# Linear attention plus SwiGLU, first four tiles: another way to transpose tiles 2 and 3, and query products summed by quarters

## The chip, the cores and the metric

The kernel runs on one core of one Trainium2 chip. A core has five engines that run side by side, each from a list of instructions of its own: TensorE (PE, matmuls and the loads of its weights, PEld), VectorE (DVE), ScalarE (ACT), GpSimd (POOL) and SyncE (SP, which here only issues DMA transfers). They wait for each other with semaphores. The metric is the device time in microseconds (us). The kernel before took 210.95 us (median of three runs, 210.83 to 211.18).

## The reference

Input x has 2048 rows of 512 numbers (bf16). It is normalised by rows, and the same normalised rows feed two blocks whose outputs are added to x.

```python
def _layernorm(x, axis=-1, eps=1e-5):
    m = jnp.mean(x, axis=axis, keepdims=True)
    v = jnp.var(x, axis=axis, keepdims=True)
    return (x - m) / jnp.sqrt(v + eps)

def _A_ref(x, wqkv, wo):                       # 32 heads of 16
    qkv = (x @ wqkv).reshape(B, S, 3, H, Dh).transpose(2, 0, 3, 1, 4)
    q, k, v = qkv[0], qkv[1], qkv[2]
    phi = lambda t: jnp.where(t > 0, t + 1, jnp.exp(t)) + 1e-6
    pq, pk = phi(q), phi(k)
    kv = jnp.einsum("bhsd,bhse->bhde", pk, v)
    z = jnp.einsum("bhsd->bhd", pk)
    num = jnp.einsum("bhqd,bhde->bhqe", pq, kv)
    den = jnp.einsum("bhqd,bhd->bhq", pq, z)[..., None] + 1e-6
    return (num / den).transpose(0, 2, 1, 3).reshape(B, S, D) @ wo

def _B_ref(x, w_gate, w_up, w_down):           # 1792 hidden
    return (jax.nn.silu(x @ w_gate) * (x @ w_up)) @ w_down

xn = _layernorm(x)
out = x + _A_ref(xn, A_wqkv, A_wo) + _B_ref(xn, B_w_gate, B_w_up, B_w_down)
```

## The kernel before, in words

The rows are cut into 16 tiles of 128, called tile 0 to 15, and the 512 columns into four chunks of 128. For the attention the kernel never forms V: it sums G = xnᵀ·phi(K) over all tiles in four PSUM banks (4 to 7) and multiplies by the V weights once at the end.

For each tile t the usual path is as follows. VectorE takes mean and variance (`bns`, L296, and `agg`, L299). 1/sqrt(var + eps) comes from two tiny operations, `eps` (L343, POOL or VectorE) and `rstd_of` (L352, POOL). `xn_dve` (L332) writes the normalised tile. A DMA transpose issued by SP (`transpose_dma`, L423) turns it, so that TensorE can use it as weights. `kproj` and `qproj` (L432) make K and Q, four matmuls of 512 columns each, into PSUM banks: bank 0 holds K and bank 1 holds Q of the even tiles, banks 2 and 3 those of the odd ones. ScalarE takes exp of K and of Q and copies Q out; VectorE clips exp K (L488) and adds max(K, 0) (L497), which gives phi(K). `gtacc` (L573) then adds xnᵀ·phi(K), four matmuls, to banks 4 to 7, and POOL adds phi(K) into a running sum (`zsum`, L565).

Tiles 0, 1 and 2 take another path, so that TensorE can begin early. Their rows are only centred (x minus mean, `xc_half` L379 or `xc_full` L389), the centred tile is transposed into `xcT`, and 1/sqrt is applied later as the scale of the ScalarE operations that read the products: `first_ek` (L505, exp), `first_pk` (L511, relu) and `first_pq` (L523, copy of Q). Scaling by a positive number per row after the product is the same as before it. Tiles 0 and 1 are transposed on TensorE against an identity (`tp_first`, L407: two transposes for half a tile, then one ScalarE copy from PSUM, L416). Tile 2 is transposed by a DMA (`transpose_xc`, L398). `proj_first` (L446) multiplies half the chunks at a time: halves 0 and 1 hold chunks 0, 1 and 2, 3. phi(K) of these tiles is the sum of two SBUF tensors, on POOL for tile 0 (`feat_pool`, L530) and on VectorE for tiles 1 and 2 (`first_feat`, L537). Exp of Q of tiles 0 to 2 is made in iterations 11 to 13 (`late_eq`, L517), and their normalised tiles are transposed by DMA in iterations 7 to 9, for the feed-forward block.

The order of the work is written out by hand. Every helper appends one operation to the list of its engine, with the semaphores that its inputs and outputs need, so the order of the calls is the order on each engine, and an operation that waits holds up everything behind it on that engine. Lines 593 to 700 hold the order for tiles 0 to 4, and a loop over tiles 5 to 15 the rest; then come the 56 steps of the feed-forward block (`ffn`, L753, gate and up products) with the attention's last products and the output tiles (L925 and L936) between them. TensorE starts with eight matmuls on constants (`fill`, L268). Loads are issued from SP in the order x 0, wk chunks 0 and 1, wk 2, x 2, wq 0, wq 1, x 3, wq 2, wq 3, x 4, x 5, and from ScalarE's queue x 1 and wk 3; x 6 to 15 follow in pairs.

Of the kernel before, what the change touches and what calls it, by code (L numbers as in the profile page):

```python
# [7 lines left out]
ALU = mybir.AluOpType  # L8
AX = mybir.AxisListType

P = 128
# [97 lines left out]
def bass_parallel_sum__linear_attn_block__swiglu_ffn__prompt_kernel(  # L109
# [16 lines left out]
    with contextlib.ExitStack() as es:  # L126
# [7 lines left out]
        xc_sb = sb("xc_sb", [3, D])  # L134
        xcT = sb("xcT", [3 * NDC, P])
# [123 lines left out]
        xload("sp", sp, 5, 1)  # L259

# [40 lines left out]
        def mean_act(t):  # L301
            K.op(
                "act",
                lambda: act.activation(
                    scr[:, :], x_sb[:, t, :], ACT.Copy, scale=1.0 / D, accum_out=mact[:, t, :],
                ),
                r=[("x", t)], w=[("mact", t), ("scr",)],
            )

        def negmean(t):  # L310
            K.op(
                "pool",
                lambda: pool.tensor_scalar(
                    out=nb[:, t:t + 1], in0=mv[:, t, 0:1], scalar1=rstd[:, t:t + 1], scalar2=-1.0,
                    op0=ALU.mult, op1=ALU.mult,
                ),
                r=[("mv", t), ("rstd", t)], w=[("nb", t)],
            )

        def xn_act(t):  # L320
            K.op(
                "act",
                lambda: act.activation(
                    xn_sb[:, t, :], x_sb[:, t, :], ACT.Identity, scale=rstd[:, t:t + 1], bias=nb[:, t:t + 1],
                ),
                r=[("x", t), ("nb", t), ("rstd", t)], w=[("xn", t)],
            )
# [74 lines left out]
        def tp_first(t, h, b):  # L402
# [10 lines left out]
            )  # L413
            K.op(
# [26 lines left out]
        def proj_first(t, wname, h):  # L441
# [10 lines left out]
                r=[("xcT", t, h)] + [(wname, i) for i in ((2, 3) if h else (0, 1))], w=[bk(b)],  # L452
            )
# [49 lines left out]
        def first_ek(t):  # L503
            K.op(
                "act", lambda: act.activation(ek[:, t, :], banks[kb(t)], ACT.Exp, scale=rstd[:, t:t + 1]),  # L505
                r=[bk(kb(t)), ("rstd", t)], w=[("ek", t)],
            )

        def first_pk(t):
            K.op(  # L510
                "act", lambda: act.activation(kpos[:, t, :], banks[kb(t)], ACT.Relu, scale=rstd[:, t:t + 1]),  # L511
                r=[bk(kb(t)), ("rstd", t)], w=[("kpos", t)],
            )
# [13 lines left out]
        def feat_pool(t):  # L527
            K.op(
                "pool",
                lambda: pool.tensor_tensor(out=pkq[:, t, 0, :], in0=kpos[:, t, :], in1=ek[:, t, :], op=ALU.add),  # L530
                r=[("kpos", t), ("ek", t)], w=[("pk", t)],
            )

        def first_feat(t):
            K.op(
                "dve",
                lambda: dve.tensor_tensor(out=pkq[:, t, 0, :], in0=kpos[:, t, :], in1=ek[:, t, :], op=ALU.add),  # L537
                r=[("kpos", t), ("ek", t)], w=[("pk", t)],
# [55 lines left out]
        stat(0)  # L594
        negmean(0)
        mean_act(1)
        xc_half(0, 0)
        tp_first(0, 0, 4)
        xc_half(0, 1)
        tp_first(0, 1, 5)  # L600
        fill(1, P)
        xc_half(1, 0, mact[:, 1, :], "mact")
        tp_first(1, 0, 6)
        xc_half(1, 1, mact[:, 1, :], "mact")
        tp_first(1, 1, 7)
        proj_first(0, "wk", 0)
        proj_first(0, "wk", 1)
        first_ek(0)
        bns(1)
        agg(1)  # L610
        eps(1, "pool")
        bns(2)
        agg(2)
        xc_full(2)
        proj_first(1, "wk", 0)
        proj_first(1, "wk", 1)
        first_pk(0)
        rstd_of(1)
        first_ek(1)
        clip_k(0)  # L620
        proj_first(0, "wq", 0)
        feat_pool(0)
        bns(3)
        agg(3)
        eps(3, "dve")
        rstd_of(3)
        proj_first(1, "wq", 0)
        xn_act(0)
        proj_first(0, "wq", 1)
        first_pq(0)  # L630
        bns(4)
        agg(4)
        eps(4, "pool")
        proj_first(1, "wq", 1)
        xn_dve(3)
        clip_k(1)
        xn_dve(1)
        gtacc(0)
        transpose_xc(2)
        proj_first(2, "wk", 0)  # L640
        proj_first(2, "wk", 1)
        xload("sp", sp, 6, 2)
        proj_first(2, "wq", 0)
        proj_first(2, "wq", 1)
        first_pk(1)
        first_feat(1)
        gtacc(1)
        rstd_of(4)
        xn_dve(4)
        bns(5)  # L650
        agg(5)
        first_pq(1)
        eps(2, "pool")
        rstd_of(2)
# [3 lines left out]
        transpose_dma(3)  # L658
        kproj(3)
        qproj(3)  # L660
        rstd_of(5)
        transpose_dma(4)
        xload("sp", sp, 8, 2)
        xn_dve(2)
        first_pk(2)
        first_feat(2)
        gtacc(2)
        xn_dve(5)
        xload("sp", sp, 10, 2)
        bns(6)  # L670
        exp_k(3)
        clip_k(3)
        agg(6)
        eps(6, "pool")
        rstd_of(6)
        transpose_dma(5)
        xload("sp", sp, 12, 2)
        xload("sp", sp, 14, 2)
        zsum(0, 0)
        bns(7)  # L680
        first_pq(2)
        copy_q(3)
        maxadd_k(3)
        kproj(4)
        xn(6)
        exp_k(4)
        qproj(4)
        agg(7)
        eps(7, "pool")
        exp_q(3)  # L690
        rstd_of(7)
        exp_q(4)
        copy_q(4)
        clip_k(4)
        stat(8)
        xn(7)
        zsum(1, 1)
        maxadd_k(4)
        stat(9)
# [6 lines left out]
        for t in range(5, NT):  # L706
# [12 lines left out]
            if t in (7, 8, 9):  # L719
                transpose_dma(t - 7)  # L720
# [6 lines left out]
            if t in (11, 12, 13):  # L727
                late_eq(t - 11)
# [304 lines left out]
```

## Time and profile before

| what | value |
|---|---|
| runs, device time | 210.83, 210.95, 211.18 us (median 210.95) |
| the profiled execution's own time | 210.89 us |
| its span, first to last instruction | 209.7 us |
| TensorE busy | 206.7 us (99%), 983 matmuls and transposes |
| VectorE, ScalarE, POOL busy | 119.4 (57%), 70.2 (33%), 74.4 (35%) us |
| share of the last chain of work on TensorE | 95% |
| granted TensorE clock, mean | 1.0 |

Rows of the timeline read: start and length in us, engine (PE, PEld, DVE, ACT, POOL, or a queue such as SPq that issues a DMA), line of the kernel, operation, output<-inputs, partitions x elements and type, xcount of like instructions in a row, and in brackets the idle time of the engine before them with what ended it. Lengths of matmuls overlap in time, because one starts before the last of the one ahead has drained: what one costs is read from the starts of two neighbours. For a DMA the issue is the row, and the landing is told apart from it.

### The profile page before, as it was taken

To read this page: it belongs to the slowest core of one execution; us is meant where nothing else is said; L and a number is where in the kernel's file an instruction comes from. 1 tells how busy PE (TensorE), PEld (TensorE's weight loads), DVE (VectorE), ACT (ScalarE), POOL (GpSimd) and SP (SyncE) were. 2 spreads that over 40 slices of the span, in tenths; PEclk is the share of its full clock that TensorE was granted. 3 is DMA by queue.
4 is the path that set the end of the run, shared out by engine and by line. 5 is a ranking of instruction groups with operands and counts; after the bars stand their busy time and mean duration, and the time that the engine had idled before them with its cause. 6 is when DMAs were issued, how large, how long until landed. Compare 5 with 4: busy or idle time off the path is not lost.

```text
span 209.7 us, 2763 instructions
## 1 busy us (share of the span) xinstructions
PE 206.7 (99%) x983; PEld 94.7 (45%) x983; DVE 119.4 (57%) x243; ACT 70.2 (33%) x123; POOL 74.4 (35%) x96
## 2 busy tenths in 40 slices
PE   8999999999999999999999999999999999999996
PEld 3344444445444444444444444444444444444444
DVE  4899988336265774637355746365556535373222
ACT  5957667956633331302122312213031213121000
POOL 3648987567032443223141422240424132221200
DMA  6766344894791111010202110202021010410201
GB/s 204 196 182 172 69 88 100 276 363 138 218 347 34 22 28 26 27 25 28 50 2 50 25 28 25 50 0 50 4 49 25 27 25 25 49 30 27 50 25 53
DMA packets 30287, 16.84 MB, mean 80 GB/s; under 512 B 20928, under 2 KB 29632, under 8 KB 30272
## 3 DMA queue, kind: packets, MB, share of 16 engines
q1 hardware_dynamic: 29984, 16.39, 29.6%
q10 hardware_dynamic: 288, 0.26, 0.4%
q8 instruction: 8, 0.13, 0.3%
q14 instruction: 7, 0.06, 0.1%
HBM read 9.70 MB, written 2.10 MB: 56 GB/s over the span
## 4 chain that ended last, share of the span: by engine, by line
PE 95%; DMA 2%; SPq 2%; issue 0%; DVE 0%
PE psum L753 46%; PE psum L936 23%; PE psum L432 11%; PE psum L925 7%; PE psum L573 7%; DMA wqkv_sb<-in_A_wqkv_dram 2%; PE psum L446 1%; SPq L211 1%; SPq L204 1%; PE psum L851 0%; PE psum L874 0%; DVE out_sb L949 0%
## 5 line engine op out<-in xcount | busy, mean ns | idle before, releaser
L768 ACT ACTIVATE sg<-psum 128x512 bf16<-128x512 f32 x56 | 33.4, 598 | 106.8 <-PE psum L753 104.9
L753 PE MATMUL psum<-xnT,wg_sb 128*128 128x512 bf16 x224 | 57.5, 379 | 0.0
L753 PE MATMUL psum<-xnT,wu_sb 128*128 128x512 bf16 x224 | 57.5, 379 | 0.0
L883 POOL TENSOR_TENSOR prod<-pkq,zb 128x512 f32<-128x512 bf16 x16 | 18.6, 1161 | 57.7 <-DVE pkq L497 57.7
L753 PEld LDWEIGHTS psum<-xnT,wu_sb 128*128 128x128 bf16 x224 | 21.9, 98 | 26.4
L753 PEld LDWEIGHTS psum<-xnT,wg_sb 128*128 128x128 bf16 x224 | 21.9, 98 | 26.2
L949 DVE TENSOR_TENSOR out_sb<-psum,x_sb 128x512 bf16<-128x512 f32 (+2 forms) x17 | 11.2, 660 | 35.5 <-PE psum L936 35.5
L907 POOL TENSOR_TENSOR pqn<-pkq,rden 128x512 bf16<-128x512 bf16 x16 | 16.9, 1056 | 36.9 <-DVE rden L901 36.9
L774 DVE TENSOR_TENSOR pkq<-psum,sg 128x512 bf16<-128x512 f32 x28 | 19.1, 687 | 18.5 <-PE psum L753 14.0
L774 DVE TENSOR_TENSOR xn_sb<-psum,sg 128x512 bf16<-128x512 f32 x28 | 18.8, 673 | 14.9 <-PE psum L753 14.4
L936 PE MATMUL psum<-wd_sb,xn_sb 128*128 128x512 bf16 (+2 forms) x126 | 25.7, 355 | 0.0
L936 PE MATMUL psum<-wd_sb,pkq 128*128 128x512 bf16 x112 | 25.5, 379 | 0.0
L432 PE MATMUL psum<-wqkv_sb,xnT 128*128 128x512 bf16 x104 | 24.4, 379 | 0.0
L565 POOL TENSOR_TENSOR zacc<-zacc,pkq 128x512 f32<-128x512 f32 x15 | 17.3, 1156 | 5.0 <-DVE ek L488 4.6
L936 PEld LDWEIGHTS psum<-wd_sb,xn_sb 128*128 128x128 bf16 x126 | 11.8, 98 | 12.5
L936 PEld LDWEIGHTS psum<-wd_sb,pkq 128*128 128x128 bf16 x112 | 11.0, 98 | 13.2
L925 PE MATMUL psum<-m_sb,eq 128*128 128x512 bf16 (+2 forms) x68 | 16.6, 366 | 0.0
L573 PE MATMUL psum<-pkq,xn_sb 128*128 128x512 bf16 x64 | 16.1, 379 | 0.0
L432 PEld LDWEIGHTS psum<-wqkv_sb,xnT 128*128 128x128 bf16 x104 | 10.1, 98 | 12.3 <-ACT ek L505 0.3
L891 DVE TENSOR_REDUCE den<-prod 128x32 f32<-128x512 f32 x16 | 10.9, 684 | 5.4 <-POOL prod L883 5.3
L296 DVE BATCH_NORM_STATS2 stats<-x_sb 128x6 f32<-128x512 bf16 x16 | 10.9, 683 | 3.3 <-DMA x_sb<-in_A_x_dram 3.3
L497 DVE SCALAR_TENSOR_TENSOR pkq<-pkq,eq 128x512 bf16<-128x512 bf16 x16 | 11.1, 693 | 0.6
(65 smaller groups left out, 136.7 us busy)
## 6 DMA issues: line engine op xcount, KB each, us to landing
out_dram<-out_sb SPq DMA_DIRECT2D x15, 128.0 KB, 1.7
wg_sb<-in_B_w_gate_dram SPq DMA_DIRECT2D x2, 896.0 KB, 7.8
wu_sb<-in_B_w_up_dram SPq DMA_DIRECT2D x2, 896.0 KB, 6.1
wd_sb<-in_B_w_down_dram SPq DMA_DIRECT2D x1, 1792.0 KB, 9.8
x_sb<-in_A_x_dram SPq DMA_DIRECT2D x5, 256.0 KB, 3.0
x_sb<-in_A_x_dram SPq DMA_DIRECT2D x5, 128.0 KB, 3.3
wqkv_sb<-in_A_wqkv_dram SPq DMA_DIRECT2D x5, 128.0 KB, 3.5
wqkv_sb<-in_A_wqkv_dram SPq DMA_DIRECT2D x1, 512.0 KB, 7.8
```

The lines of the kernel that those rows point to most:

```text
L432: (lambda c=c: pe.matmul(banks[b], xnT[:, c, t * P:(t + 1) * P], wqkv_sb[:, c, lo:lo + D], start=(c == 0), stop=(c == NDC - 1),))
L497: lambda: dve.scalar_tensor_tensor(out=dst, in0=src, scalar=0.0, in1=e, op0=ALU.max, op1=ALU.add,),
L565: lambda: pool.tensor_tensor(out=zacc[:, :], in0=zacc[:, :], in1=pk, op=ALU.add),
L573: (lambda c=c: pe.matmul(banks[4 + c], xn_sb[:, t, c * P:(c + 1) * P], pkq[:, t, 0, :], start=(t == 0), stop=(t == NT - 1),))
L753: (lambda c=c: pe.matmul(banks[b], w_sb[:, c, fc * P:(fc + 1) * P], xnT[:, c, C * 512:(C + 1) * 512], start=(c == 0), stop=(c == NDC - 1),))
L768: lambda: act.activation(sg[:, j % NSG, :], banks[gb], ACT.Silu),
L774: lambda: dve.tensor_tensor(out=hT(C, fc), in0=banks[ub], in1=sg[:, j % NSG, :], op=ALU.mult,),
L883: lambda: pool.tensor_tensor(out=p, in0=pkq[:, t, 1, :], in1=zb[:, :], op=ALU.mult),
L907: lambda: pool.tensor_tensor(out=pqn[:, t % NPN, :].rearrange("p (h e) -> p h e", e=DH), in0=pkq[:, t, 1, :].rearrange("p (h e) -> p h e", ...
L925: (lambda g=g: pe.matmul(dst, pqnT(t)[:, g, :], m_sb[:, g, lo:hi], start=(g == 0), stop=False,))
L936: (lambda fc=fc: pe.matmul(dst, hT(C, fc)[:, jj * P:(jj + 1) * P], wd_sb[:, fc, lo:hi], start=False, stop=(fc == NFC - 1),))
L949: lambda: dve.tensor_tensor(out=o, in0=src, in1=x_sb[:, t, lo:hi], op=ALU.add),
```

## The change

It touches the written-out order of tiles 0 to 4 and some helpers.

- Tile 3 goes the way of tiles 0 to 2: centred, transposed by DMA into `xcT`, multiplied with `proj_first`, its 1/sqrt applied by `first_ek`, `first_pk`, `first_pq`. Its normalised tile is still made, and its DMA transpose moves to iteration 6 of the loop; its exp of Q moves to iteration 14.
- Tile 2 is transposed on TensorE (banks 4 and 5) instead of by DMA. The ScalarE copy becomes a helper of its own (`tc_first`).
- Q 0 and Q 1, and K 0 and K 1, are issued one matmul at a time (`proj_part`): K by chunks 0, 1, 3, 2. After chunks 0 and 1 of Q 1 and of Q 0 stand the four transposes of tile 2, then chunk 2 of Q 0 and Q 1, chunk 3 of Q 0 and, behind it, chunk 3 of Q 1.
- Tile 0 is normalised on VectorE instead of ScalarE, and the small product on POOL for its bias goes.
- The load of x 6 and 7 is issued right behind x 5, before any transpose. `gtacc` 0 moves behind Q 2, `gtacc` 1 and 2 behind K 3, and the order on ScalarE, VectorE and POOL changes with them.

```diff
-        xc_sb = sb("xc_sb", [3, D])
-        xcT = sb("xcT", [3 * NDC, P])
+        xc_sb = sb("xc_sb", [4, D])
+        xcT = sb("xcT", [4 * NDC, P])
...
         xload("sp", sp, 5, 1)
+        xload("sp", sp, 6, 2)
...
+        def tc_first(t, h, b):
+            tb = banks[b].bitcast(bf)[:, 0:HD].rearrange("p (c s) -> p c s", c=2)
             K.op(
                 "act",
                 lambda: act.activation(xcT[:, NDC * t + 2 * h:NDC * t + 2 * h + 2, :], tb, ACT.Copy),
...
+        def proj_part(t, wname, c, pos):
+            lo, b = (D, kb(t)) if wname == "wk" else (0, qb(t))
+            K.op(
+                "pe",
+                lambda: pe.matmul(
+                    banks[b], xcT[:, NDC * t + c, :], wqkv_sb[:, c, lo:lo + D],
+                    start=(pos == 0), stop=(pos == NDC - 1),
+                ),
+                r=[("xcT", t, c // 2), (wname, c)], w=[bk(b)],
+            )
...
         fill(8, 512)
-        stat(0)
-        negmean(0)
+        bns(0)
+        agg(0)
+        xc_half(0, 0)
+        xc_half(0, 1)
         mean_act(1)
-        xc_half(0, 0)
+        xc_half(1, 0, mact[:, 1, :], "mact")
+        xc_half(1, 1, mact[:, 1, :], "mact")
         tp_first(0, 0, 4)
-        xc_half(0, 1)
+        tc_first(0, 0, 4)
+        fill(1, P)
         tp_first(0, 1, 5)
-        fill(1, P)
-        xc_half(1, 0, mact[:, 1, :], "mact")
+        tc_first(0, 1, 5)
+        eps(0, "pool")
         tp_first(1, 0, 6)
-        xc_half(1, 1, mact[:, 1, :], "mact")
+        tc_first(1, 0, 6)
+        bns(1)
+        rstd_of(0)
+        xn_dve(0)
         tp_first(1, 1, 7)
-        proj_first(0, "wk", 0)
-        proj_first(0, "wk", 1)
-        first_ek(0)
-        bns(1)
         agg(1)
-        eps(1, "pool")
+        tc_first(1, 1, 7)
         bns(2)
         agg(2)
-        xc_full(2)
...
+        xc_half(2, 0)
+        xc_half(2, 1)
+        bns(3)
+        agg(3)
+        proj_part(0, "wk", 0, 0)
+        proj_part(0, "wk", 1, 1)
+        proj_part(0, "wk", 3, 2)
+        proj_part(0, "wk", 2, 3)
+        first_ek(0)
+        clip_k(0)
+        xc_full(3)
+        bns(4)
+        eps(3, "dve")
+        proj_part(1, "wk", 0, 0)
...
+        proj_part(1, "wq", 0, 0)
+        proj_part(1, "wq", 1, 1)
+        transpose_xc(3)
+        xload("sp", sp, 8, 2)
+        proj_part(0, "wq", 0, 0)
+        proj_part(0, "wq", 1, 1)
         first_pk(0)
+        tp_first(2, 0, 4)
+        tc_first(2, 0, 4)
+        tp_first(2, 1, 5)
+        tc_first(2, 1, 5)
+        agg(4)
+        bns(5)
+        proj_part(0, "wq", 2, 2)
+        proj_part(1, "wq", 2, 2)
+        proj_part(0, "wq", 3, 3)
+        first_pq(0)
+        eps(2, "pool")
+        rstd_of(2)
+        proj_part(1, "wq", 3, 3)
+        proj_first(2, "wk", 0)
+        proj_first(2, "wk", 1)
+        eps(1, "pool")
         rstd_of(1)
         first_ek(1)
...
+        clip_k(1)
+        first_pq(1)
         xn_dve(1)
-        gtacc(0)
-        transpose_xc(2)
-        proj_first(2, "wk", 0)
-        proj_first(2, "wk", 1)
-        xload("sp", sp, 6, 2)
         proj_first(2, "wq", 0)
         proj_first(2, "wq", 1)
+        feat_pool(0)
+        gtacc(0)
+        eps(4, "pool")
+        rstd_of(4)
+        xn(4)
+        xload("sp", sp, 10, 2)
+        agg(5)
         first_pk(1)
         first_feat(1)
...
+        proj_first(3, "wk", 0)
         first_ek(2)
         clip_k(2)
         eps(5, "dve")
-        transpose_dma(3)
-        kproj(3)
-        qproj(3)
...
         xn_dve(2)
+        proj_first(3, "wq", 0)
+        proj_first(3, "wq", 1)
         first_pk(2)
         first_feat(2)
-        gtacc(2)
-        xn_dve(5)
-        xload("sp", sp, 10, 2)
+        rstd_of(3)
+        rstd_of(5)
+        xn(5)
+        xload("sp", sp, 12, 2)
+        xload("sp", sp, 14, 2)
         bns(6)
-        exp_k(3)
+        first_pq(2)
+        proj_first(3, "wk", 1)
+        first_ek(3)
         clip_k(3)
+        zsum(0, 0)
+        first_pk(3)
         agg(6)
         eps(6, "pool")
+        first_feat(3)
+        gtacc(1)
+        gtacc(2)
+        xn_dve(3)
+        bns(7)
+        kproj(4)
         rstd_of(6)
...
-            if t in (7, 8, 9):
-                transpose_dma(t - 7)
+            if t in (6, 7, 8, 9):
+                transpose_dma((3, 0, 1, 2)[t - 6])
...
-            if t in (11, 12, 13):
+            if t in (11, 12, 13, 14):
                 late_eq(t - 11)
```

## The prediction

> **What bounds the kernel now.** I read the page's busy times first, then what TensorE waited for, then its timeline, and last the timelines of the engines and queues that feed it around the edits. The page, its first lines:
>
> ```profile
> span 209.7 us, 2763 instructions
> ## 1 busy us (share of the span) xinstructions
> PE 206.7 (99%) x983; PEld 94.7 (45%) x983; DVE 119.4 (57%) x243; ACT 70.2 (33%) x123; POOL 74.4 (35%) x96
> ```
>
> The view of waits, TensorE alone, over the whole span (waited for; us in total, times, longest):
>
> ```profile
> PE psum L268 <- PEq L1018: 0.8, 1, 0.8
> PE psum L446 <- DMA wqkv_sb<-in_A_wqkv_dram: 0.3, 1, 0.3
> ```
>
> So TensorE is the bound, and between its first instruction and its last it stands still once, for a load of weights. Its timeline shows where (start, length, line, count, idle before):
>
> ```profile
> 4.21 0.62 PE L407 MATMUL psum<-ident,xc_sb 128*128 128x128 bf16 x4
> ...
> 4.72 0.39 PE L407 MATMUL psum<-ident,xc_sb 128*128 128x128 bf16 x4
> 5.10 2.76 PE L446 MATMUL psum<-wqkv_sb,xcT 128*128 128x512 bf16 x12
> 8.13 1.04 PE L446 MATMUL psum<-wqkv_sb,xcT 128*128 128x512 bf16 x4 [0.27 <-DMA wqkv_sb<-in_A_wqkv_dram]
> 9.01 1.03 PE L573 MATMUL psum<-pkq,xn_sb 128*128 128x512 bf16 x4
> 9.87 1.89 PE L446 MATMUL psum<-wqkv_sb,xcT 128*128 128x512 bf16 x8
> 11.60 1.03 PE L573 MATMUL psum<-pkq,xn_sb 128*128 128x512 bf16 x4
> 12.46 1.89 PE L432 MATMUL psum<-wqkv_sb,xnT 128*128 128x512 bf16 x8
> ```
>
> Matmuls overlap: four of 512 columns start 9.01 and the next group 9.87, so one costs 0.216 us, though its row lasts 0.379. The four transposes at 4.72 end 0.39 later and last 0.22 each, so they start 0.056 apart. The last of the twelve matmuls starts at 7.486 and leaves the array free at 7.702; the next starts at 8.135. The real hole is thus 0.433 us, not the printed 0.27. From 8.135 to 207.83 starts follow each other without a hole. Whatever is done to tiles 0 to 3 can win back at most this 0.433 us, and loses one us per us of any new hole, since nothing behind it has slack to take it up.
>
> What fills the feeding engines there (the timeline of all engines; q marks a queue that issues):
>
> ```profile
> 4.12 0.91 SPq L211 DMA_DIRECT2D wqkv_sb<-in_A_wqkv_dram  x2
> ...
> 6.89 0.35 DVE L389 TENSOR_SCALAR xc_sb<-x_sb,mv 128x512 bf16<-128x512 bf16 x1
> ...
> 7.27 1.28 SPq L398 DMA_TRANSPOSE xcT<-xc_sb  x1
> ...
> 7.90 0.82 ACT L323 ACTIVATE xn_sb<-x_sb,nb,rstd 128x512 bf16<-128x512 bf16 x1
> ...
> 8.60 0.57 SPq L204 DMA_DIRECT2D x_sb<-in_A_x_dram  x1
> ...
> 8.78 0.69 ACT L523 ACTIVATE pkq<-psum,rstd 128x512 bf16<-128x512 f32 x1
> ...
> 9.80 1.47 PEld L446 LDWEIGHTS psum<-wqkv_sb,xcT 128*128 128x128 bf16 x8 [0.26 <-DMA xcT<-xc_sb]
> ...
> 14.03 1.19 SPq L423 DMA_TRANSPOSE xnT<-xn_sb  x1
> 15.27 1.05 SPq L204 DMA_DIRECT2D x_sb<-in_A_x_dram  x2
> 15.97 0.59 DVE L332 TENSOR_SCALAR xn_sb<-x_sb,mv,rstd 128x512 bf16<-128x512 bf16 x1
> ```
>
> The last two chunks of wq are issued at 4.12 and 4.60 and take 3.5 to land: 7.67 and 8.09. Second use: the DMA transpose of tile 2 is issued at 7.27, 0.03 after its data, and its weights load at 9.80: 2.5 from issue to landing.
>
> **The change, part by part, walked on TensorE's clock.** Nothing before 5.10 changes: the same eight fills, eight transposes and one small fill stand there (the fill one place later), the same statistics, and the same four copies on ScalarE (4.66 to 5.87). I keep 5.102 for the first K matmul.
>
> *Quarters and the hole.* K 0, K 1, Q 1 (chunks 0, 1) and Q 0 (0, 1) are the same twelve matmuls, ending at 7.702; their order 0, 1, 3, 2 for wk meets weights that landed by 4.9. Now tile 2's four transposes come: 4 x 0.056 = 0.222, to 7.924. Their input, xc of tile 2 in two halves, is ready at 6.89 + 0.20 + 0.28 = 7.37 (halves start 0.20 apart at 3.75). Then Q 0 c2 and Q 1 c2 (7.67 landed), 8.356 Q 0 c3 and 8.572 Q 1 c3 (8.09 landed): no wait. The last ends at 8.788, where before it was 9.009. So the hole's 0.433 goes and 0.222 of new work stands in its place: -0.211.
>
> *Tile 2 on PE instead of a DMA.* It adds four transposes (counted) and two copies on ScalarE: 0.384 each, 0.28 apart, 8.01 to 8.68, behind first_pk 0, which ends 7.44. K 2 starts at 8.788 and needs them at 8.40 and 8.68: hidden by the last two quarters. Q 2 at 9.65 overwrites the bank that first_pq 0 reads; that starts when Q 0 is summed (8.356 + 0.379), at 8.78 as before, and ends at 9.47; release to weight load takes 0.05 (5.05 to 5.10 in the copies of tile 0). Margin about 0.1 us.
>
> *Tile 0's normalisation* leaves ScalarE (0.82) and POOL (nb, 0.27) for VectorE (0.41, between bns 1 and agg 1). VectorE stood idle for 0.50 there until x of tile 2 landed at 5.92: hidden. If x came earlier it would push xc of tile 2 by at most 0.41, to 7.78: 0.08 late.
>
> *gtacc 0* moves behind Q 2, to 10.51. The add on POOL that it needs now stands behind eps 2, rstd 2, eps 1 and rstd 1; at 0.22 to 0.51 and 0.55 to 0.65 a piece from 6.9 these end at 8.8 to 9.2, the add (1.16) at 9.9 to 10.4. Margin 0.1 to 0.6.
>
> *Tile 3 centred.* VectorE: bns 3 from 7.29 (x landed 7.24), agg 3 to 8.20, clip 0, then xc 3 from 8.33 to 8.69. SP then has only the x 6-7 load in front, issued behind x 5 at 6.0; the transpose issues at 8.72 and lands at 11.20 by the 2.5 of tile 2's. K 3 wants it at 11.37 (Q 2 to 10.51, gtacc 0 to 11.37). It also wants bank 2 free: on ScalarE pq 0, ek 1, pq 1, pk 1 start 0.58 apart from 8.78, so pk 1 ends at 11.21. Both margins are about 0.1, and these are the tightest of the change. The x 6-7 load's own traffic is through long before: it is queued behind x 5, landed 8.74, and tiles of 128 KB landed 0.3 to 0.4 apart, so its two are through by about 9.5, while the transpose's data move some 1.3 after its issue, when the issue itself ends, at 10.0.
>
> *Behind it.* K 3, Q 3: 11.37 to 13.10, then gtacc 1 and 2 (to 14.83), K 4, Q 4 (to 16.56), gtacc 3. The last inputs: first_feat 1 at 12.0 for 13.10; first_feat 2 at 13.2 for 13.97; xnT of tile 4, whose transpose is issued at 11.3, 2.6 later at 13.9 for 14.83; first_feat 3 and xn 3 at 15.3 and 15.6 for 16.56; maxadd 4 at 18.6 for gtacc 4 at 19.15 (before 18.8 for 19.37). VectorE's additions in the stretch, xn 0 (0.41), xc 3 (0.35) and a half (0.13), are 0.9; they take the places of its idle 0.50, 0.42 and 0.15. ScalarE's added relu of tile 3 (0.68) falls in gaps of 1.06, 0.64 and 0.93.
>
> *SP and late work.* The transpose of xn 3 moves to iteration 6 (1.27 of SP). SP stood idle 0.97 between 23.61 and 24.58 and 0.42 ahead of 30.12, so the transposes behind it slip 0.3 and the FFN weight loads at 36.59 do not. If they slipped by the whole 1.27, the first half of wu would land at 45.4 for a use at 47.6: still nothing. The late exp of tile 3 (0.63) sits in a 0.69 idle of ScalarE.
>
> The sum against the profiled execution, 210.89 (span 209.7 and 1.2 around it): 210.89 - 0.433 + 0.222 = 210.68. That execution is 0.06 under the median of 210.95, so I expect a median of 210.74. The price not shown is that of switching TensorE from 512-column matmuls to transposes and back: by the sixteen 128-column matmuls at L851 (0.056 each, among matmuls) nothing; by the row length of a warm transpose, were they not overlapped, 4 x 0.219 = 0.88. I take nothing, the nearer row.
>
> One rule speaks against the change. The Trainium skill, page "VectorE: DVE Perf Modes", section "The three transpose paths", prices a TensorE transpose of 128x128 bf16 at 390 ns; charged one after the other, four would be an estimated 1.56 in place of 0.22, and the sum 212.0. The trace does not bear this out: at 4.72 four were through in 0.39.
>
> **The rivals.**
> *Transposes not overlapped* (0.88 by the row above): 210.74 + 0.66 = 211.4. Against it, the starts 0.056 apart. Chance 0.03. By the figure of the Trainium skill's page named above this rival would give 212.0; the trace shows no transpose that long.
>
> *Tile 3's transpose a little late.* The point is landing at 11.3, 2.6 after issue. The transpose at 14.03 ran beside x loads and took 2.85, others 3.0: landings at 11.6 to 11.7, hole 0.25 to 0.4, total 211.0 to 211.15, level with before. For it: VectorE's two-operand scalings stretch beside POOL (0.59 at 15.97, beside a cast, against 0.41), and xc 3 runs beside rstd 1; that alone adds up to 0.2. Chance 0.16.
>
> *Tile 3's transpose very late: slower.* The longest of the trace, issued at 18.25, took 4.0. From 8.72 it would land at 12.76, hole 1.4, total 212.1. It decides from a landing at 11.95 on (hole 0.65, total 211.37). Against it: that one was queued behind four tiles of x, here only two, already moved. Similar size: if the traffic of x 6-7, now issued at 6.0, shared the engines with wq, the quarters would wait 0.4 and xc's transpose too. Together 0.17.
>
> *More gained than the hole*, for instance a first K matmul before 5.10: nothing moved stands there. 0.05, 210.5 or less.
>
> **How the numbers follow.** Dense after the quarters: 0.59, 210.6 to 210.9 by the scatter of the runs (-0.12, +0.23). Little late 0.16, very late 0.17, transposes 0.03, more gained 0.05. Predicted 210.74. The range runs from 210.5 to 211.4, which leaves out the very late case (0.17) and a few hundredths at the low end. A change under 0.2% (0.42 us) is about what a measurement can tell from none here; the forecast, -0.1%, lies inside. Within 0.2%: 0.59 + 0.16 = 0.75; slower: 0.17 + half of 0.03 = 0.19; faster: 0.06, the rest.
>
> **What would show it.** Right: no wait of TensorE on wqkv_sb; four transposes in 0.39 at about 7.7; Q 0's last quarter at 8.4; K 3 at 11.37 directly behind gtacc 0; end of the last matmul 0.21 earlier. Wrong: a gap before K 3 that ends on xcT or on kpos, one before Q 2 that ends on pkq, or before gtacc 0 on POOL; or starts 0.2 apart in the new transposes.

## The result, and the profile after

The changed kernel took 212.39 us (median of ten runs, 211.43 to 213.08) against 210.95 us of the kernel before (ten runs, 210.68 to 211.57). The ratio is 1.0058, with a 95% interval of 1.0042 to 1.0074: slower by about 1.2 us by the ratio (the medians lie 1.44 apart), where 0.2 us less was forecast, and outside the range of 210.5 to 211.4. Its profiled execution took 212.38 us, 1.49 us more than that of before. (Line numbers of the changed kernel differ: its DMA transposes are L408, the K and Q products of later tiles L417, those of the first tiles L431 and L444, the PE transposes L389, gtacc L569.)

The first lines of its page:

```profile
span 211.1 us, 2755 instructions
...
PE 206.5 (98%) x968; PEld 95.3 (45%) x987; DVE 119.6 (57%) x246; ACT 70.9 (34%) x125; POOL 74.2 (35%) x95
```

TensorE is still the bound, but what it waited for is another thing. The view of its waits:

```profile
PE psum L269 <- PEq L1036: 0.8, 1, 0.8
PE psum L417 <- DMA xnT<-xn_sb: 0.8, 1, 0.8
```

The wait for wq is gone, and a wait for a DMA transpose has come. TensorE's timeline shows both, and a third thing, at the start:

```profile
4.54 0.40 PE L389 MATMUL psum<-ident,xc_sb 128*128 128x128 bf16 x2
...
5.48 3.13 PE L444 MATMUL psum<-wqkv_sb,xcT 128*128 128x512 bf16 x12
8.44 0.39 PE L389 MATMUL psum<-ident,xc_sb 128*128 128x128 bf16 x4
8.66 1.03 PE L444 MATMUL psum<-wqkv_sb,xcT 128*128 128x512 bf16 x4
9.53 1.89 PE L431 MATMUL psum<-wqkv_sb,xcT 128*128 128x512 bf16 x8
11.26 1.03 PE L569 MATMUL psum<-pkq,xn_sb 128*128 128x512 bf16 x4
12.33 1.67 PE L431 MATMUL psum<-wqkv_sb,xcT 128*128 128x512 bf16 x7
...
19.89 1.03 PE L569 MATMUL psum<-pkq,xn_sb 128*128 128x512 bf16 x4
21.71 0.60 PE L417 MATMUL psum<-wqkv_sb,xnT 128*128 128x512 bf16 x2 [0.80 <-DMA xnT<-xn_sb]
```

From 8.44 to 20.54 starts follow each other without a hole, as forecast (K 3's eighth record is missing at 12.12; the place is exactly one matmul wide). Then K 6, whose turn is at 20.75, starts at 21.71: 0.96 us lost. And the twelve matmuls from 5.48 end later than before: the last of them starts at 8.226 instead of 7.486. So the first tile's part came 0.74 us late: the first tile of x landed at 3.23 instead of 2.78, and matmuls of 512 columns started 0.427 apart until 6.28, where the profile before has 0.216 from the first K on.

The sum closes: 210.89 - 0.433 (hole) + 0.222 (transposes) + 0.74 (start) + 0.96 (K 6) = 212.38.

What K 6 waited for is tile 6's transpose. Its issue alone, and what DMA queues moved between 19.4 and 20.6 us (queue and kind: packets, MB, share):

```profile
L408 SPq DMA_TRANSPOSE xnT<-xn_sb x1: 1198/1198/1198, 17.6 to 17.6; - x1
...
  PE psum L417: 0.8, 1
DMA to landing us min/median/max: 4.0/4.0/4.0
```

```profile
q1 hardware_dynamic: 265, 0.06, 25.2%
q8 instruction: 1, 0.02, 5.4%
```

It was issued at 17.63 and landed at 21.67, 4.04 later, where most transposes take 2.4 to 3.0. A single packet of queue 8, of kind "instruction" and 16 KB, began at 19.50 and took 1.04 us on one DMA engine. By its kind it is the program's own code on its way. At its beginning 488 of the transpose's 512 data packets had started, 19 more followed by 19.65, and the last five, by the count, came only after it. In the profile before, such a packet came at 20.12, when tile 6's transpose had landed (issued 16.59, landed 19.58); tile 7's, in flight then, took 4.04 as well, and nobody waited for it, since K 7's turn came at 22.8. That was the 4.0 of the prediction.

### The profile page after: what moved, and what is told of

The parts are those of the page before. It is cut to its first block, busy times and chain, and to the rows that moved or that the text cites. A ratio compares the mean times of both kernels' runs of the same rounds, so it can differ in the third digit from the quotient of the medians.

```text
span 211.1 us, 2755 instructions
## 1 busy us (share of the span) xinstructions
PE 206.5 (98%) x968; PEld 95.3 (45%) x987; DVE 119.6 (57%) x246; ACT 70.9 (34%) x125; POOL 74.2 (35%) x95
## 4 chain that ended last, share of the span: by engine, by line
PE 89%; DVE 4%; DMA 3%; ACT 2%; issue 1%; POOL 1%; DVEq 0%
PE psum L771 44%; PE psum L954 23%; PE psum L417 8%; PE psum L943 7%; PE psum L569 4%; DMA xnT<-xn_sb 2%; PE psum L444 2%; DMA x_sb<-in_A_x_dram 1%; DVE pkq L533 1%; ACT ek L501 1%; ACT pkq L519 1%; PE psum L389 1%; DVE stats L297 1%; ACT kpos L507 1%; POOL prod L901 1%
## 5 line engine op out<-in xcount | busy, mean ns | idle before, releaser
L771 PE MATMUL psum<-xnT,wu_sb 128*128 128x512 bf16 x217 | 56.0, 379 | 0.4
L901 POOL TENSOR_TENSOR prod<-pkq,zb 128x512 f32<-128x512 bf16 x16 | 18.6, 1160 | 57.8 <-DVE pkq L493 57.8
L792 DVE TENSOR_TENSOR pkq<-psum,sg 128x512 bf16<-128x512 f32 x28 | 19.1, 687 | 18.6 <-PE psum L771 14.1
L417 PE MATMUL psum<-wqkv_sb,xnT 128*128 128x512 bf16 x94 | 22.3, 379 | 0.9 <-DMA xnT<-xn_sb 0.8
L569 PE MATMUL psum<-pkq,xn_sb 128*128 128x512 bf16 x63 | 15.9, 379 | 0.1
L417 PEld LDWEIGHTS psum<-wqkv_sb,xnT 128*128 128x128 bf16 x96 | 9.3, 98 | 12.4 <-DMA xnT<-xn_sb 1.3
```

The source lines that it names most:

```text
L417: (lambda c=c: pe.matmul(banks[b], xnT[:, c, t * P:(t + 1) * P], wqkv_sb[:, c, lo:lo + D], start=(c == 0), stop=(c == NDC - 1),))
L569: (lambda c=c: pe.matmul(banks[4 + c], xn_sb[:, t, c * P:(c + 1) * P], pkq[:, t, 0, :], start=(t == 0), stop=(t == NT - 1),))
L771: (lambda c=c: pe.matmul(banks[b], w_sb[:, c, fc * P:(fc + 1) * P], xnT[:, c, C * 512:(C + 1) * 512], start=(c == 0), stop=(c == NDC - 1),))
L792: lambda: dve.tensor_tensor(out=hT(C, fc), in0=banks[ub], in1=sg[:, j % NSG, :], op=ALU.mult,),
L901: lambda: pool.tensor_tensor(out=p, in0=pkq[:, t, 1, :], in1=zb[:, :], op=ALU.mult),
```

## The experiments

The theories. F: a transpose that is on the DMA engines while a block of instructions is fetched lands late, and the change brought tile 6's transpose and the fetch together. L: the new order on VectorE simply makes tile 6 too late. S: the start varies from run to run, and the kernel before hides a part of that in its hole, while the changed kernel has no hole left.

One table for all profiles; times in us from the span's start. "First x" is the landing of the first tile of x, "full pace" when matmuls begin to start 0.216 (or 0.056) apart, "K 6 waits" what the start of K 6 lies behind its turn. The ratio is to the kernel before.

| profile | first x | first K | full pace | tile 6 issued | fetch | tile 6 landed | K 6 waits | its time | ratio (95%) |
|---|---|---|---|---|---|---|---|---|---|
| before | 2.78 | 5.10 | 4.7 | 16.59 | 20.12 | 19.58 | 0 | 210.89 | 1 |
| before, again | 3.20 | 5.28 | 4.8 | 16.68 | 20.44 | 20.17 | 0 | 210.99 | - |
| changed | 3.23 | 5.48 | 6.3 | 17.63 | 19.50 | 21.67 | 0.96 | 212.38 | 1.0058 (1.0042 to 1.0074) |
| changed, again | 3.10 | 5.35 | 6.2 | 17.52 | 19.36 | 21.48 | 0.88 | 212.19 | 1.0053 (1.0038 to 1.0069) |
| changed, 32 short fills | 3.21 | 5.46 | 5.8 | 17.35 | 18.21 | 20.99 | 0.57 | 211.70 | 1.0030 (1.0017 to 1.0042) |
| changed, tile 6 early | 3.24 | 5.49 | 6.7 | 16.93 | 19.71 | 21.73 | 0.74 | 212.44 | 1.0059 (1.0039 to 1.0078) |
| changed, loads later | 3.18 | 5.25 | 4.6 | 17.48 | 18.38 | 20.76 | 0.27 | 212.31 | 1.0062 (1.0046 to 1.0079) |
| changed, both | 3.12 | 5.30 | 5.1 | 16.22 | 18.59 | 18.63 | 0 | 210.97 | 1.0012 (0.9996 to 1.0027) |
| both, loads behind tile 7 | 3.18 | 5.43 | 7.0 | 17.02 | 19.37 | 19.43 | 0 | 211.98 | 1.0021 (1.0008 to 1.0035) |
| both, and delay | 3.21 | 5.84 | 6.6 | 17.03 | 19.24 | 19.45 | 0 | 212.34 | 1.0063 (1.0042 to 1.0084) |
| before, delay | 3.05 | 5.69 | 6.1 | 17.25 | 20.80 | 20.53 | 0 | 211.44 | 1.0016 (1.0004 to 1.0028) |
| before, fills cut | 3.19 | 5.44 | 6.2 | 17.14 | 19.59 | 21.93 | 1.30 | 212.64 | 1.0067 (1.0050 to 1.0083) |
| before, more fill | 3.22 | 5.65 | 6.4 | 17.40 | 19.89 | 21.94 | 1.05 | 212.65 | 1.0072 (1.0057 to 1.0086) |
| before, tile 2 on PE | 3.29 | 5.37 | 4.9 | 16.73 | 19.61 | 21.85 | 1.57 | 212.57 | 1.0089 (1.0055 to 1.0122) |

**The changed kernel again, nothing altered.**

> The changed kernel once more, nothing altered. In its first profile two things stood: the first K matmul ran 0.4 us later than in the kernel before and the next ones on the slow clock until 6.3 us (0.74 us in all), and K 6 waited 0.96 us for the DMA transpose of tile 6, which took 4.04 us from issue to landing. Theory F (an instruction fetch of 16 KB, at 19.5 us, holds one of the DMA engines while tile 6's transpose is on them): the fetch and the 4 us landing come again, hole at K 6 0.7 to 1.1 us. Theory L (tile 6 is simply normalised too late by the new order): the hole comes again, with or without a fetch beside it. Theory S (the late start is chance, and the kernel before hides it in its hole of 0.43 us): the first x tile lands at another time, 2.8 to 3.3 us, and the total moves with it. Total 211.5 to 213, slower than the kernel before by 0.5 to 1.5 us.

All of it came again: fetch 19.36, tile 6's transpose 3.96 us, K 6 waits 0.88. So the wait belongs to the kernel. What the first tile of x did in the first profile of before, 2.78, came in none of the thirteen others (3.05 to 3.29).

**The kernel before again, nothing altered.**

> The kernel before, nothing altered, for a second profile. Theory S (the lucky start was in its first profile, where the first tile of x landed 2.8 us in; in five other profiles it landed at 3.1 to 3.2): the first tile lands at about 3.2, the first K matmul runs at 5.3 to 5.5, the slow clock lasts to about 6.2, and the hole ahead of the last chunks of wq shrinks from 0.43 to 0.1 us or less, so that the total is only 0 to 0.4 us longer. The rival, that the start depends on the kernel: landing at 2.8, hole 0.43, total 210.9. Both: tile 6's transpose lands 3 us after its issue and K 6 does not wait.

TensorE's timeline:

```profile
4.52 0.48 PE L407 MATMUL psum<-ident,xc_sb 128*128 128x128 bf16 x4 [0.43 <-DVE xc_sb L379]
5.28 2.76 PE L446 MATMUL psum<-wqkv_sb,xcT 128*128 128x512 bf16 x12
8.23 1.04 PE L446 MATMUL psum<-wqkv_sb,xcT 128*128 128x512 bf16 x4 [0.19 <-DMA wqkv_sb<-in_A_wqkv_dram]
9.11 1.03 PE L573 MATMUL psum<-pkq,xn_sb 128*128 128x512 bf16 x4
```

The first tile of x landed at 3.20, so the 2.78 of the first profile was a lucky start. But the full pace was there at once, at 4.8, and the hole ahead of Q 0 was still 0.355 (the last start of the twelve at 7.66, plus one matmul of 0.216, to 8.233). The first K came 0.18 later than in the first profile, the hole was 0.08 shorter and gtacc 0 started 0.10 later, as the sum asks. Total 210.99. S is right on the landing and too strong on the hole: a late landing alone uses little of it up, and only a slow pace uses it up whole.

**The fetch moved in the changed kernel.**

```diff
-        fill(8, 512)
+        fill(32, P)
```

> The changed kernel with the eight opening matmuls of 512 columns cut into 32 of 128: the same 3.4 us of filling, but 24 matmuls and 24 weight loads more in TensorE's list, so its next block of instructions is fetched some 5 us earlier, at about 14 us, when tile 4's transpose has landed and tile 5's has not begun. Theory F: tile 6's transpose lands 2.5 to 3.0 us after its issue, no hole at K 6, total 0.8 to 1.0 us below the unaltered changed kernel. Theory L: tile 6's transpose still lands behind K 6's turn, hole about 0.9 us, total unchanged.

A miss in part. The fetch moved by 1.2 us, not by 5 (why so little is open), and still met tile 6's transpose: it landed 3.64 us after its issue, at 20.99 instead of the 21.48 of the second profile of the changed kernel. K 6 waited 0.57 instead of 0.88, and the time fell by 0.5: 0.3 of it from this wait, and 0.2 from the start, where the full pace came at 5.8. The wait went with the fetch, though the issue hardly moved (17.52 to 17.35), which speaks for F; but L is not out by this run.

**The fetch moved in the kernel before.**

```diff
-        fill(8, 512)
+        fill(6, 512)
+        fill(8, P)
```

> The kernel before with two of its eight opening matmuls of 512 columns cut into eight of 128: the same time of filling, but 12 instructions more in TensorE's list, so the fetch of 16 KB moves from 20.1 us to about 18.9 us, where tile 6's transpose is on the DMA engines (it was issued at 16.6 and landed at 19.6). Theory F: that transpose now lands 3.5 to 4.1 us after its issue, at 20.1 to 20.7, and K 6, whose turn is at 20.2, waits up to 0.6 us; total 211.0 to 211.6. Theory L: no hole, 210.95 as before.

This run decides between F and L. Not an instruction of VectorE, ScalarE, POOL or SP was touched, and of TensorE only the opening matmuls on constants. TensorE's timeline:

```profile
19.81 1.03 PE L573 MATMUL psum<-pkq,xn_sb 128*128 128x512 bf16 x4
21.98 1.25 PE L432 MATMUL psum<-wqkv_sb,xnT 128*128 128x512 bf16 x5 [1.14 <-DMA xnT<-xn_sb]
```

Tile 6's transpose, and the instruction queue between 19.5 and 20.8 us:

```profile
DMA to landing us min/median/max: 4.8/4.8/4.8
```

```profile
q8 instruction: 1, 0.02, 5.6%
```

The kernel before, with its own order, now has the changed kernel's wait, longer even: tile 6's transpose took 4.80 and K 6 waited 1.30; ratio 1.0067. L cannot have this, since nothing made tile 6 later but the start, by 0.46. Nor does a late start alone do it: in the kernel before with the delay (below), whose TensorE list is untouched, gtacc 0 started as late (9.57 against 9.46), the fetch came at 20.80, tile 6's transpose had landed at 20.53, and K 6 did not wait. The size was forecast at 0.6 at most, less than half of what came.

**Four more opening matmuls in the kernel before.**

```diff
         fill(8, 512)
+        fill(4, P)
```

> The kernel before with four more opening matmuls of 128 columns, 0.43 us of filling on the slow clock, so that TensorE is busy until the first tile is centred also when x lands at 3.2 us. If the idle 0.1 to 0.3 us ahead of the first transposes is what keeps the clock slow until 6.2: full clock from about 4.7, first K at 5.3, total 0 to 0.3 us below the kernel before. If the clock's change has its own time: no gain, +0 to 0.2. Theory F adds: eight instructions more ahead of the fetch bring it onto tile 6's transpose, and K 6 waits 0.3 to 1.3 us, total 211.5 to 212.5.

The filling did not bring the full pace forward (6.4), and TensorE had no idle time ahead of the first transposes here, so such idle time is not what kept the pace slow. The fetch came at 19.89 onto the transpose: 4.54 us, K 6 waits 1.05.

**One part alone: tile 2 on TensorE.**

```diff
         proj_first(1, "wq", 0)
-        xn_act(0)
+        tp_first(2, 0, 4)
+        tp_first(2, 1, 5)
         proj_first(0, "wq", 1)
         first_pq(0)
+        xn_act(0)
...
-        gtacc(0)
-        transpose_xc(2)
         proj_first(2, "wk", 0)
...
         proj_first(2, "wq", 1)
+        gtacc(0)
```

> One part alone: the kernel before with tile 2 transposed on TensorE between the first two and the last two chunks of Q 0 and Q 1 (four transposes, two ScalarE copies, the ScalarE normalisation of tile 0 behind the first copy of Q, gtacc 0 behind Q 2); tile 3 keeps its old way, and no product is cut into quarters. Theory S: at the usual start the hole is gone already, and the four transposes cost +0.22 us; a forecast from the first profile alone says -0.21. Theory F: eight instructions more ahead of the fetch bring it forward by 0.5 to 0.9 us, to about 19.5, onto tile 6's transpose, which then lands 3.5 us or more after its issue and makes K 6 wait 0.3 to 1.3 us: total 211.5 to 212.5. Without that collision 211.2.

```profile
5.37 2.76 PE L446 MATMUL psum<-wqkv_sb,xcT 128*128 128x512 bf16 x12
7.96 0.39 PE L407 MATMUL psum<-ident,xc_sb 128*128 128x128 bf16 x4
8.19 2.75 PE L446 MATMUL psum<-wqkv_sb,xcT 128*128 128x512 bf16 x12
...
21.90 1.47 PE L432 MATMUL psum<-wqkv_sb,xnT 128*128 128x512 bf16 x6 [1.41 <-DMA xnT<-xn_sb]
```

The part does at 7.96 what it is for: four transposes in the place of the hole. And by itself it makes the loss: fetch at 19.61, tile 6's transpose 5.12 us, K 6 waits 1.57, ratio 1.0089. Against the second profile of before the sum closes: 210.99 + 0.09 (first K) - 0.355 (hole) + 0.222 + 0.05 (a wait at 12.3) + 1.57 = 212.57, as measured. So tile 3's new way is not needed for the loss.

**Tile 6 early, the loads later, and both.** On VectorE and POOL tile 6's statistics go ahead of tile 3's clip, and its normalisation ahead of tile 3's:

```diff
         bns(6)
+        agg(6)
+        eps(6, "pool")
+        rstd_of(6)
...
         first_feat(3)
...
+        xn_dve(6)
+        transpose_dma(6)
         xn_dve(3)
```

> The changed kernel with tile 6's aggregate ahead of tile 3's clip on VectorE, its two small POOL operations ahead of the first running sum, and its normalisation ahead of tile 3's, so that its transpose is issued at about 16.5 instead of 17.6 us. Theories F and L both: it lands by 19.6, before the fetch and before K 6's turn at 20.7; the hole at K 6 goes, total 0.8 to 1.0 us below the changed kernel. A third theory, that the x loads of tiles 12 to 15 ahead of it in the queue hold it up, expects that it still lands 3.5 us or more after its issue, and a hole of 0 to 0.3 us.

F's and L's forecasts both missed. The issue moved by 0.7, to 16.93, and the landing not at all: 21.73, 4.80 after it. The loads of x 12 to 15, issued from 15.62 on, landed at 18.98 and 19.69. The transpose's data moved late, from 18.6 to 19.7, and were just ending when the fetch came at 19.71; the last of its four-byte writes came at 20.68, when the packet was nearly through. So the issue (L) does not set the landing; and the loads alone, without a packet, made no transpose of a tile longer than 3.5 in any profile. The next run left the order of VectorE alone and moved the loads:

```diff
         xn(5)
-        xload("sp", sp, 12, 2)
-        xload("sp", sp, 14, 2)
...
         transpose_dma(6)
+        xload("sp", sp, 12, 2)
+        xload("sp", sp, 14, 2)
```

> The changed kernel with the loads of x 12 to 15 behind tile 6's transpose instead of ahead of it, and nothing else: the transpose is still issued at about 17.5. Theory F: its data move at 18.6 to 19.4, the fetch comes at 18.6 to 19.5, it lands 3.5 us or more after its issue at 21.0 to 21.7, K 6 waits 0.3 to 0.9 us, total 211.6 to 212.4. If the loads ahead of it are the cause: landing 2.5 us after issue, at 20.0, no wait, total 211.2 to 211.5.

Tile 6's transpose took 3.28 and K 6 waited 0.27, between the two forecasts. Its turn itself was late: gtacc 4, just ahead of it, had waited 0.36 for phi(K) from VectorE, so the landing at 20.76 was 0.6 behind the place that K 6 would have had. And the loads were now ahead of tile 7's transpose: it took 3.91, with a smaller instruction packet of 8 KB at 22.34 while it was in flight, and K 7 waited 0.84. Which of the two made it late, the run does not separate. The total did not move. Both edits together, on SP's queue:

```diff
         xn(5)
-        xload("sp", sp, 12, 2)
-        xload("sp", sp, 14, 2)
...
+        xn_dve(6)
+        transpose_dma(6)
+        xload("sp", sp, 12, 2)
+        xload("sp", sp, 14, 2)
         xn_dve(3)
```

> The changed kernel with tile 6's normalisation early (as in the run that only moved that) and, in addition, the loads of x 12 to 15 behind tile 6's transpose instead of ahead of it. Theory F: the transpose is issued at about 16.5, moves its data by 18.3, lands at about 19, ahead of the fetch at 19.4 to 19.7; K 6 does not wait; total 0.8 to 1.0 us below the changed kernel, 211.2 to 211.5. Then what is left against the kernel before is the price of four transposes without a hole to stand in, +0.2 us at the usual start (theory S). If the late transposes had another cause than the fetch, K 6 still waits 0.5 us or more.

```profile
5.30 2.76 PE L444 MATMUL psum<-wqkv_sb,xcT 128*128 128x512 bf16 x12
7.91 0.39 PE L389 MATMUL psum<-ident,xc_sb 128*128 128x128 bf16 x4
8.13 1.03 PE L444 MATMUL psum<-wqkv_sb,xcT 128*128 128x512 bf16 x4
...
20.32 1.89 PE L417 MATMUL psum<-wqkv_sb,xnT 128*128 128x512 bf16 x8
```

Tile 6's transpose was issued at 16.22 and landed at 18.63, 2.41 later, just as the fetch began (18.59), and no wait of K 6 is left. Time 210.97 in the profile. Against the second profile of before, which has the same start and pace: 210.99 + 0.02 (first K) - 0.355 + 0.222 + 0.09 (a wait of gtacc 4 at 19.4) = 210.97. So in this execution, where nothing waits on a transpose, the change and the two edits gain 0.04 us: 0.13 from the hole less the transposes, of which the early normalisation takes 0.09 back (gtacc 4 has this wait in each run with that edit, and not in the unaltered changed kernel). Its eleven runs fall in two groups, seven from 210.93 to 211.28 and four from 212.03 to 212.20. What the slower group waits for is open, since the profile is of the faster one; tile 7's transpose behind the loads is a candidate. The next run puts the loads behind tile 7's transpose too:

```diff
         transpose_dma(6)
-        xload("sp", sp, 12, 2)
-        xload("sp", sp, 14, 2)
...
         xn(7)
+        xload("sp", sp, 12, 2)
+        xload("sp", sp, 14, 2)
```

> The changed kernel with tile 6 normalised early and the loads of x 12 to 15 behind tile 7's transpose, so that neither transpose has a load ahead of it. Theory F: tile 6's transpose lands by 19, tile 7's, issued at 18.8, lands at 21.3, or at 22.4 if the fetch catches it, both ahead of K 7's turn at 22.9; no wait of TensorE on a transpose; total 211.0 where TensorE's clock is full by 5 us, 211.6 where it is slow until 6.2, and none at 212 or more. If late transposes come whatever the fetch and the loads do: again times at 212 and more, as in a third of the runs with the loads behind tile 6's.

Tiles 6 and 7 landed 2.41 and 2.39 after issue and no wait on a transpose of theirs is left, but two of twelve runs were still over 212 (212.34 and 212.75), and the ratio is 1.0021: no better. Tile 8's transpose was now the one behind the loads; it took 4.39, with an 8 KB packet at 24.60, and K 8 started 0.21 behind its turn. None of the versions beats the kernel before.

**Delays at the start.** Tile 0 is centred once more, in vain, which puts 0.27 us on VectorE ahead of the first transposes and adds nothing to TensorE's list:

```diff
+        xc_full(0)
         xc_half(0, 0)
```

> The kernel before with tile 0 centred once more, in one piece, ahead of its two halves on VectorE: work done twice, to make the first transposes 0.27 us later without one instruction more on TensorE, so that the fetch keeps its place in the work. Theory S: the hole ahead of the last chunks of wq (0.35 to 0.43 us in two profiles) shrinks to about 0.1 and the total stays within 0.1 us of the kernel before. If the hole is no slack (the wq chunks are waited for relative to the work, not to the clock on the wall): hole unchanged, total +0.27 us.

> The same delay of 0.27 us put into the changed kernel with tile 6's transpose cleared of the fetch (early normalisation, loads of x 12 to 15 behind it). Theory S: there is no hole left to hide it, the total rises by the whole 0.27 us against the run without the delay (210.97 in its profile, 211.19 median). If this kernel still had slack at the start: no rise.

Both missed. TensorE's timeline of the kernel before with the delay:

```profile
5.69 3.79 PE L446 MATMUL psum<-wqkv_sb,xcT 128*128 128x512 bf16 x16
9.57 1.02 PE L573 MATMUL psum<-pkq,xn_sb 128*128 128x512 bf16 x4
```

The delay met the slow pace, so the start came 0.41 later than in the second profile of before (the first K), and the first twelve matmuls ended 0.58 later. The hole is gone, as S says: sixteen matmuls in one row. But gtacc 0 then waits 0.25 for tile 0's normalised tile, which ScalarE had only at 9.47 (this row's end), behind exp and relu of K 0 and exp of K 1:

```profile
8.65 0.82 ACT L323 ACTIVATE xn_sb<-x_sb,nb,rstd 128x512 bf16<-128x512 bf16 x1
```

So of 0.58 us the hole took 0.355, and the next wait gave 0.25 back: 0.47, but for 0.01 of rounding. gtacc 0 starts 0.46 later (9.57 against 9.11), and the total is 0.45 up. The hole is slack, but only for one of the two chains that a late start pushes. In the changed kernel with the delay, TensorE's K 6 did not wait, but K 7 did (0.56; its transpose took 4.52 us, with an 8 KB packet at 22.31, and landed at 24.14, in the same moment as the end of the ScalarE copy to which the view puts the wait down), so that its time says nothing clean of 0.27.

## Why the prediction was wrong, point by point

*The hole and the quarters* were right. No wait on wq is left in any run of the changed kernel, and the four transposes start 0.056 apart (8.442 to 8.609). The Trainium skill, page "VectorE: DVE Perf Modes", section "The three transpose paths", gives 390 ns for one; four were through in 0.39 in every run, so the rival built on it is out, as the row had said.

*Tile 3 centred, gtacc 0, Q 2* were right: the DMA transpose of xc 3 took 2.49 (issued 8.92, landed 11.41) and K 3 followed gtacc 0 directly. The two rivals set on that transpose did not come. The margins that were called the tightest held: the transpose landed 0.7 ahead of K 3's turn in the changed kernel's profile, where TensorE was 0.74 late, and about 0.3 ahead in the two variants at full pace.

*"Behind it"* is the step that failed. It lists what gtacc 1 to 4 and K 4 need and stops there; tile 6's transpose is not in it. By the rows of before it would have had a margin of 0.65 (landed 19.58, K 6 at 20.23). In the changed kernel it was issued about 1.0 later (17.63 instead of 16.59). The rows that led to it, of the changed kernel:

```profile
15.76 0.65 POOL L325 TENSOR_SCALAR vpe<-mv 128x1 f32<-128x1 f32 x1
16.50 0.58 POOL L334 TENSOR_TENSOR rstd<-vpe,nhalf 128x1 f32<-128x1 f32 x1
17.19 0.41 DVE L314 TENSOR_SCALAR xn_sb<-x_sb,mv,rstd 128x512 bf16<-128x512 bf16 x1
17.63 1.20 SPq L408 DMA_TRANSPOSE xnT<-xn_sb  x1
```

and the row of before that belongs to the second of these:

```profile
15.28 0.57 POOL L352 TENSOR_TENSOR rstd<-vpe,nhalf 128x1 f32<-128x1 f32 x1
```

Tile 6's aggregate stood behind tile 3's clip on VectorE (15.02 instead of 14.71), its two small POOL operations behind the first running sum (done at 17.08 instead of 15.85), so its normalisation began at 17.19 instead of 15.97. K 6's turn came only 0.5 later, so the margin was down to 0.1 for a transpose of 3.0. That alone would have cost nothing; with the 3.50 that the same transpose took in the second profile of before, with no packet beside it, it would have cost an estimated 0.4. The rest is the fetch.

*The 4.0 us* was seen and read wrongly. The prediction put it down to four tiles of x in the queue and set the rival on tile 3's transpose. The transpose just ahead spoke against it: tile 6's, issued at 16.59 behind the same four tiles, took 2.99. Nor was 4.0 the longest of the trace: one issued at 177.32 took 4.17, with a 16 KB packet at 178.62. The page before has a row for the instruction queue, with 8 packets; when each of them moved, and beside which transpose, was not asked. In eleven profiles the transpose that was next to land when the first 16 KB instruction packet began landed 2.0 to 2.8 after that beginning, whatever its issue (tile 6's in five profiles of the changed kernel and its variants and in three of the varied kernel before, and tile 7's in the three of the kernel before as it was or only delayed). In the other three, those with both edits, it was 0.2 or less from landing and landed 2.41 to 2.43 after its issue. The Trainium skill, page "DMA: Bandwidth & Descriptors", section "Queues, rings and completion order", states that a DMA engine serves its queues in turn and switches only at the end of a packet, and that a semaphore increment lands only after every earlier write of that engine, across its queues. The trace does not name the engine of a packet, so it cannot show the first; a 16 KB packet took 0.93 to 1.46 us at this place. It agrees with the second as far as it shows: in the changed kernel 30 of the transpose's 32 four-byte writes were made by 19.67, the last two at 20.69 and 20.70, after the packet. The landing at 21.67, another microsecond on, no run explains.

*Past each queue.* The prediction counted SP's issues and engine times of what moved, but not that four transposes and their weight loads are eight more instructions in TensorE's list. With 8 and with 12 more, the kernel before had its fetch at 19.6 to 19.9 instead of 20.1 to 20.4, and lost 1.05 to 1.57 us at K 6.

*The start* was taken from one execution, and kept fixed. In fourteen profiles the first tile of x landed at 2.78 once and at 3.05 to 3.29 otherwise, and the full pace came at 4.6 to 5.1 in five and at 5.8 to 7.0 in nine, in variants of both kernels. The Trainium skill, page "TensorE: Matmul & The Clock Gate", section "Part 1", states that TensorE runs at half rate until a free-running window of 3.4 us has been busy, 426.7 and 215.7 ns per matmul of 512 columns; the traces agree in the pace (0.427 and 0.216) and show a wider spread of the moment than its 0.5 us. The profile's row of the granted clock reads 1.00 throughout and does not show this pace.

What a start costs each kernel is read from the start of the twelfth of the 512-column matmuls to the first start behind the sixteenth, with all that stands between (the hole, the transposes, a wait). The kernel before needs 1.52 in its first profile, 1.45 in its second and 1.33 in its three variants at the slow pace and with the old order (the delay, the fills cut, more fill), where the wait for wq is gone but gtacc 0 waits 0.25 for tile 0's normalised tile. The changed kernel and its variants need 1.30 in every profile in which all these records are there. So the gain of 0.211, worked out from the luckiest start, is 0.13 to 0.14 at the usual one with full pace, and 0.03 where the pace is slow. The hole could hide at most 0.19 of a late start: of the 0.74, an estimated 0.55 would have come to the kernel before too. Of the 1.49 us between the two profiles, then, the 0.96 at K 6 is the change's own price, and most of the rest is the luck of the first execution. Between the runs the mean difference is 1.2 us, some 0.3 more than K 6 explains less this gain; what that is, and how often each kernel meets the slow pace, no profile shows.

*The chances.* Slower had 0.19, and the case named for it was right in kind (a transpose of 4 us that makes TensorE wait 1.4) and wrong in its place and its cause. Had the mechanism been looked for at every transpose that TensorE waits on, tile 6's would have been the first candidate.

## What to carry to other kernels

A hole on the bounding engine can be slack for whatever varies ahead of it: before filling it, ask over several executions how much of it is there, and what the work put in it costs when it is not. When instructions are added to an engine's list or moved in it, every later DMA with a margin under 2 us is to be looked at again (the longest transpose here took 5.1 instead of 3.0), and packets of kind "instruction" are to be laid beside the transposes and loads in flight. A landing that comes far later than its neighbours' is not to be put down to the nearest traffic before the queue table has been asked which packets moved beside it, and when.

## What the runs showed of the hardware

A block of the program's own instructions, 16 KB in one packet every 17 to 32 us, can delay a DMA transpose that it meets: the eleven above took 3.3 to 5.1 us from issue to landing. The fourteen profiles hold 517 DMA transposes. The 394 with no instruction packet in flight took 2.4 to 3.7 us, 376 of them at most 3.0, and all 18 that took more than 3.7 had one in flight. A meeting does not always cost: in the changed kernel's first profile tile 7's transpose was in flight during the same packet as tile 6's, moved most of its data behind it, and took 2.97. Beside packets of 8 KB three took 3.9 to 4.5 (one of them had met the end of a 16 KB packet too), the other 43 at most 3.5.

The place of a fetch is not simply counted in instructions: 48 more ahead of it moved it by 1.2 us, 12 more by 0.5 to 0.9, 8 more by 0.2 to 0.8. With the TensorE list of the changed kernel it came at 18.4 and 18.6 in the two profiles at full pace and at 19.2 to 19.7 in the five at the slow pace. What sets it stays open.
